# One 8 MB K load per head in place of two of 4 MB, with the second half copied aside

## The chip, the cores and the metric

The kernel runs on one core of one Trainium2 chip. The metric is the device time of one execution in microseconds; a kernel is timed in several rounds beside the kernel before on the same chip. Nothing here fell in a slow state, apart from one run of the kernel before (501.61 us, in the job of the last three edits to the changed kernel), which is left out of every ratio.

## The reference, cut to what matters

A decoder block for one token: a modulated layernorm, attention with 32 query heads over 4 cached KV heads and 32768 positions for 2 batches, an output projection, then an MLP. The caches are 8 pairs (batch, KV head) of an 8 MB K and an 8 MB V, 134 MB of the 178 MB that are read. "Head" below is such a pair; heads are counted from 0 to 7.

```python
q = (x @ wq).reshape(B, Sq, Hq, Dh).transpose(0, 2, 1, 3)      # B, Sq = 2, 1; Hq, Dh = 32, 128
k = jnp.repeat(k_cache, rep, axis=1)                           # k_cache: (2, 4, 32768, 128) bf16
scores = jnp.einsum('bhqd,bhkd->bhqk', q, k) * Dh ** (-0.5)
p = _softmax(scores, axis=-1)
o = jnp.einsum('bhqk,bhkd->bhqd', p, v)                        # v from v_cache, of k_cache's shape
return o.transpose(0, 2, 1, 3).reshape(B, Sq, Hq * Dh) @ wo
```

## The kernel before

SyncE issues all loads, in a fixed order, into an arena of 160 KB per partition. For a head there are two K slots of 32 KB and one V slot of 64 KB. A load waits until everything that read the slot has finished. Within a head, K is worked through in four chunks (cc) of eight groups (g8). A group is eight PE transposes of 128 x 128 into one of four PSUM buffers, an eviction to SBUF by VectorE or ScalarE, and eight small products with q, three groups later. The maximum of the scores, the exponential and the PV product follow when all four chunks are done. The kernel's own bookkeeping enters every read of a PSUM bank as a write, so two engines that read one bank take turns, in the order in which the program names them.

```python
EVAC_PATTERN = ("dve", "act", "dve", "act", "dve", "dve", "act", "dve")
def add_k(i, hf):
    add(("K", i, hf), [2, TPC * D], A_k_cache[i % 2, i // 2].rearrange(
        "(p h c t) d -> h p c (t d)", h=2, c=2, p=128)[hf], hf * 32 * KB, f"K{hf}")
def add_v(i):
    add(("V", i), [NCH, TPC * D], A_v_cache[...]..., 64 * KB, "V")
for i in range(NBG):
    add_k(i, 0)
    add_k(i, 1)
    add_v(i)
# ...
def tr(i, cc, g8):
    it = need("K", i, cc // 2)            # the half that holds this chunk
    kt = it.view[:, cc % 2, :]...
    for jj in range(8):
        pe(... e.transpose(psKT[kq][...], w[:, t, :], ident[:, :]), reads=[it.reg, "ident"], ...)
    # evict psKT to KT_sb[g8] on ScalarE or VectorE, by EVAC_PATTERN[g8]
def qk(i, cc, g8):
    # ... eight products into the bank psS[cc % 2]; after the last group of a chunk:
    act(... copy of the bank to S_sb ..., sem=f"sc{cc}")
    dve(... maximum of the bank to m1c ...)
```

Of the kernel before, what the change touches and what calls it, by code (L numbers as in the profile page):

```python
# [6 lines left out]
ALU = mybir.AluOpType  # L7
AX = mybir.AxisListType
BF16 = mybir.dt.bfloat16
FP32 = mybir.dt.float32  # L10

B, G, S, D = 2, 4, 32768, 128
HQ = 32
HPG = HQ // G
# [5 lines left out]
NBG = B * G  # L20
# [6 lines left out]
TPC = CH_ROWS // 128  # L27
NCH = S // CH_ROWS
# [3 lines left out]
PIPE = 3  # L32
NPKT = 4
RING = 160 * 1024
AHEAD = ("sc2", "sc3", "pk", "ac")
WMOD_ITEMS = ((0, 1), (1, 4), (4, 8))
W2_ITEMS = ((0, 8, 96), (8, 16, 112), (16, 24, 128), (24, 27, 144), (27, 28, 150))
EVAC_PATTERN = ("dve", "act", "dve", "act", "dve", "dve", "act", "dve")


class Tracker:
# [161 lines left out]
    def _loop(self, eng, E, body, bounds):  # L203
        pairs = [w[1:] for op in body for w in op[1]]
        often = [p for p in dict.fromkeys(pairs) if p != (1, 0) and pairs.count(p) > 1]
        with eng.Fori(*bounds) as it:
            val = {(1, 0): it}
            for step, off in often:
                val[step, off] = eng.snap(it * step + off)

            def wait(w):
                eng.wait_ge(self.sem[w[0]], val[w[1:]] if w[1:] in val else it * w[1] + w[2])

            for op in body:
                self._emit(eng, E, op, wait)
# [18 lines left out]
def bass_adaLN_cond__gqa_block_cached__mixer_channel_mlp__decode_kernel(  # L234
# [13 lines left out]
    out: bass.AP,  # L248
):
    T = Tracker(nc)  # L250
    T.step["pe"], T.step["dve"] = 72, 14

    def sb(name, shape, dtype=FP32):
        return nc.alloc_sbuf_tensor(name, list(shape), dtype)
# [1 line left out]
    ident = sb("ident", [128, 128], BF16)  # L256
# [14 lines left out]
    abase = nc.lookup_mloc(arena).addr  # L271
# [30 lines left out]
    m1c = sb("m1c", [128, HPG, NCH])  # L302
# [16 lines left out]
    psKT = [nc.alloc_psum_tensor(f"psKT{i}", [128, 1024], BF16) for i in range(NPKT)]  # L319
# [10 lines left out]
    stream = []  # L330
    by_key = {}
    views = {}
    KB = 1024

    def add(key, shape, src, off, slot=None):
        it = Item()
        it.key, it.n = key, len(stream)
        it.off, it.nbytes = off, int(np.prod(shape)) * 2
        assert off + it.nbytes <= RING
        it.reg = f"it{it.n}"  # L340
        it.sem = f"d_{slot or it.reg}"
        it.view = views.get(slot)
        if it.view is None:
            it.view = nc.alloc_sbuf_tensor_at(f"{key[0]}_{it.n}", [128] + list(shape), BF16, offset=abase + off)
            if slot:
                views[slot] = it.view
        it.src = src
        stream.append(it)
        by_key[key] = it

    def add_k(i, hf):
        add(("K", i, hf), [2, TPC * D], A_k_cache[i % 2, i // 2].rearrange("(p h c t) d -> h p c (t d)", h=2, c=2, p=128)[hf], hf * 32 * KB, f"K{hf}")

    def add_v(i):
        add(("V", i), [NCH, TPC * D], A_v_cache[i % 2, i // 2].rearrange("(p c t) d -> p c (t d)", c=NCH, p=128), 64 * KB, "V")
# [6 lines left out]
    for m in range(2):  # L362
        add(("wq", m), [4, HQ * D], wq_v[:, 4 * m:4 * m + 4, :], (96 + 32 * m) * KB)
    for i in range(NBG):
        add_k(i, 0)
        add_k(i, 1)
        add_v(i)
    for m, off in enumerate((128, 0)):
        add(("wo", m), [16, DM], A_wo[m * 2048:(m + 1) * 2048, :].rearrange("(p j) n -> p j n", j=16), off * KB)
    w1_v = B_w1.rearrange("(p k) n -> p k n", k=KT8)  # L370
    for m, off in enumerate((32, 64)):
        add(("w1", m), [4, F], w1_v[:, 4 * m:4 * m + 4, :], off * KB)
    w2_v = B_w2.rearrange("(p j) n -> p j n", j=FT)
    for m, (j0, j1, off) in enumerate(W2_ITEMS):
        add(("w2", m), [j1 - j0, DM], w2_v[:, j0:j1, :], off * KB)
    w2_of = {j: (m, j - j0) for m, (j0, j1, off) in enumerate(W2_ITEMS) for j in range(j0, j1)}

    pos = [0]

    def need(*key):  # L380
        it = by_key[key]
        while pos[0] <= it.n:
            cur = stream[pos[0]]
            old = [o.reg for o in stream[:cur.n] if o.off < cur.off + cur.nbytes and cur.off < o.off + o.nbytes]
            if len(cur.view.shape) == 3:
                dst = cur.view[:, :, :]
            else:
                dst = cur.view[:, :]
            T.dma("sp", lambda e, dst=dst, src=cur.src: e.dma_start(dst, src), key=cur.sem, writes=[cur.reg], frees=old)
            pos[0] += 1  # L390
        return it


    def dve(fn, reads=(), writes=(), sem=None):
        T.inst("dve", fn, reads=reads, writes=writes, sem=sem)

    def act(fn, reads=(), writes=(), sem=None):
        T.inst("act", fn, reads=reads, writes=writes, sem=sem)
# [16 lines left out]
    for k in range(KT8):  # L415
        pe(lambda e, k=k: e.matmul(psM[:, 2 * k:2 * k + 2], lhsT=c2[:, k::KT8], rhs=ident[0:2, 0:2], start=True, stop=True),
           reads=["KT_sb0", "ident"], writes=["psM"], mark=False)
# [46 lines left out]
    for k in range(KT8):  # L464
        k0, kk = wmod_of[k]
        it = need("wmod", k0)
        for ch in range(12):
            n, q = ch // 4, ch % 4
            pe(lambda e, w=it.view, k=k, kk=kk, ch=ch, n=n, q=q: e.matmul(bank[n][32 * q:32 * q + 32, :], lhsT=inT[:, k, :], rhs=w[:, kk, ch * 512:(ch + 1) * 512],  # L469
                                                                   start=(k == 0), stop=(k == KT8 - 1), skip_group_check=True),  # L470
               reads=[it.reg, "inT"], writes=[breg[n]], mark=(ch % 4 == 3))
# [6 lines left out]
    for n in range(3):  # L478
        for i in range(4):
            lo = 32 * n + 2 * i  # L480
            pe(lambda e, n=n, i=i, lo=lo: e.matmul(psM[:, lo:lo + 32].rearrange("p (q r) -> p q r", r=8)[:, :, 0:2],
                                                   lhsT=row[:, n * 512 + i * 128:n * 512 + (i + 1) * 128], rhs=idf, start=True, stop=True),
               reads=[f"mrow{n}", "identf"] + ROW, writes=["psM"], mark=(i == 3))
# [19 lines left out]
    for k in range(KT8):  # L503
        it = need("wq", k // 4)
        for ch in range(8):
            n, q = ch // 4, ch % 4
            pe(lambda e, w=it.view, k=k, ch=ch, n=n, q=q: e.matmul(bank[n][32 * q:32 * q + 32, :], lhsT=inT[:, k, :], rhs=w[:, k % 4, ch * 512:(ch + 1) * 512],
                                                                   start=(k == 0), stop=(k == KT8 - 1), skip_group_check=True),
               reads=[it.reg, "inT"], writes=[breg[n]], mark=(ch % 4 == 3))
    act(lambda e: e.activation(qrow[:, 0:512], bank[0][:, :], ACT.Copy), reads=[breg[0]], writes=["qrow0"] + EREG)  # L510
    dve(lambda e: e.tensor_copy(qrow[:, 512:1024], bank[1][:, :]), reads=[breg[1]], writes=["qrow1"] + EREG)
    for n in range(2):
        for i in range(4):
            pe(lambda e, n=n, i=i: e.matmul(psM[:, 0:64].rearrange("p (b h) -> p h b", b=2)[:, 16 * n + i:16 * n + 16:4, :],
                                            lhsT=qrow[:, n * 512 + i * 128:n * 512 + (i + 1) * 128], rhs=idr, start=True, stop=True),
               reads=[f"qrow{n}", "ident"] + EREG, writes=["psM"], mark=(i == 3))
    dve(lambda e: e.tensor_copy(qT[:, :, :], psM[:, 0:64].rearrange("p (b h) -> p b h", b=2)), reads=["psM"], writes=["qT"], sem="mo")

    for name in AHEAD:
        T.key(name, T.step.get(name, 1))  # L520
        T.raw("pe", lambda e, name=name: e.sem_inc(T.sem[name], T.step.get(name, 1)))
    T.wait("pe", reads=["ident", "identf", "onesf", "hmat"], writes=["psS0", "psS1", "psO", "psM"] + [f"psKT{q}" for q in range(NPKT)])

    pipe = []
# [3 lines left out]
        T.inst("pool", lambda e: e.tensor_copy(qcur[:, :], qT[:, b, g * HPG:(g + 1) * HPG]), reads=["qT"] + [f"atT{g}" for g in range(G // 2)], writes=["qcur"], sem="qc")  # L528

    def tr(i, cc, g8):  # L530
        it = need("K", i, cc // 2)
        kt = it.view[:, cc % 2, :].rearrange("p (t d) -> p t d", d=D)
        kq = g8 % NPKT
        for jj in range(8):
            t = g8 * 8 + jj
            pe(lambda e, kq=kq, jj=jj, w=kt, t=t: e.transpose(psKT[kq][:, jj * 128:(jj + 1) * 128], w[:, t, :], ident[:, :]),  # L536
               reads=[it.reg, "ident"], writes=[f"psKT{kq}"], mark=(jj == 7))
        src = psKT[kq][:, :].rearrange("p (a n) -> p a n", a=8)
        if EVAC_PATTERN[g8] == "act":
            act(lambda e, src=src: e.activation(KT_sb[g8][:, :, :], src, ACT.Copy), reads=[f"psKT{kq}"], writes=[f"KT_sb{g8}"], sem=f"ev{cc}_{g8}")  # L540
        else:
            dve(lambda e, src=src: e.tensor_copy(KT_sb[g8][:, :, :], src), reads=[f"psKT{kq}"], writes=[f"KT_sb{g8}"], sem=f"ev{cc}_{g8}")  # L542

    def qk(i, cc, g8):
        ps, preg = psS[cc % 2], f"psS{cc % 2}"
        for jj in range(8):
            t = g8 * 8 + jj
            pe(lambda e, t=t, jj=jj: e.matmul(ps[:, t * HPG:(t + 1) * HPG], lhsT=KT_sb[g8][:, jj, :], rhs=qcur[:, :], start=True, stop=True),  # L548
               reads=[f"KT_sb{g8}", "qcur"], writes=[preg], mark=(jj == 7))
        if g8 == TPC // 8 - 1:  # L550
            Sc = S_sb[:, :, cc * TPC:(cc + 1) * TPC]
            act(lambda e: e.activation(Sc, ps.rearrange("p (t h) -> p h t", h=HPG), ACT.Copy), reads=[preg], writes=[f"S_sb_{cc}"], sem=f"sc{cc}")  # L552
            dve(lambda e: e.tensor_reduce(m1c[:, :, cc], ps.rearrange("p (t h) -> p h t", h=HPG), AX.X, ALU.max), reads=[preg], writes=[f"m1c{cc}"])  # L553

    def softmax_1():
        dve(lambda e: e.tensor_reduce(m1[:, :], m1c[:, :, :], AX.X, ALU.max), reads=[f"m1c{cc}" for cc in range(NCH)], writes=["m1"], sem="m1")  # L556
# [62 lines left out]
    for i in range(NBG):  # L619
        T.segments = rounds[i + 1] = {E: [] for E in T.LOOPED}  # L620

        for cc in range(NCH):
            for g8 in range(TPC // 8):
                tr(i, cc, g8)
                pipe.append((i, cc, g8))
                if (cc, g8) == (0, 0):
                    next_q(i)
                if len(pipe) > PIPE:
                    qk(*pipe.pop(0))
        while pipe:  # L630
            qk(*pipe.pop(0))
        softmax_1()
        softmax_2()
        softmax_3()
        for cc in range(NCH):
            exp(cc)
        for cc in range(NCH):
            part_sum(cc)
            pv(i, cc)
        row_sums()  # L640
        extract()
        extract_2(i)
        T.segments = None
# [6 lines left out]
    for m in range(2):  # L650
        it = need("wo", m)
        for j in range(16):
            for hf in range(2):
# [3 lines left out]
                   reads=[it.reg, f"atT{m}"], writes=["psS0"], mark=(j == 15 and hf == 1))  # L657
# [27 lines left out]
    for q in range(4):  # L685
        for n in range(2):
# [3 lines left out]
               reads=["b1m", "ident"], writes=[zreg[n]], mark=False)  # L690
    for k in range(KT8):
        it = need("w1", k // 4)
        for n in range(2):
            for q in range(4):
                lo = 896 * q + 448 * n
                pe(lambda e, w=it.view, k=k, n=n, q=q, lo=lo: e.matmul(zbank[n][32 * q:32 * q + 32, 0:448], lhsT=inT[:, k, :], rhs=w[:, k % 4, lo:lo + 448],
                                                                       start=False, stop=(k == KT8 - 1), skip_group_check=True),
                   reads=[it.reg, "inT"], writes=[zreg[n]], mark=(q == 3))
        if k == 1:
            pe(lambda e: e.matmul(psM[:, 44:52], lhsT=b2m[:, :], rhs=ident[0:KT8, 0:KT8], start=True, stop=True),  # L700
               reads=["b2m0", "b2m1", "b2m3", "b2m7", "ident"], writes=["psM"])
# [3 lines left out]
        reads=["psS1", "psO"], writes=["zrow"] + ROW)  # L705
# [3 lines left out]
        reads=["z2", "zrow"] + ROW, writes=["z2"])  # L709
# [5 lines left out]
    for g in range(16):  # L715
        m, j = w2_of[g]
        it = need("w2", m)
        for hf in range(2):
            t = 2 * (g % 2) + hf
# [5 lines left out]
    for g in range(16, FT):  # L725
        m, j = w2_of[g]
# [46 lines left out]
```

## Time and profile before

| what | value |
|---|---|
| median time | 420.12 us (420.05 to 420.14, 3 runs) |
| span of the profiled run | 418.7 us |
| busy: PE, VectorE, ScalarE | 70%, 50%, 36% |
| loads | 178.28 MB, the queue busy 98.8% |
| V landing to the next V landing | 38.7 us |

The main lines stand in the prediction. Four more are needed later. The first two are groups of instructions, with count, busy time and mean duration in ns, then idle time before them; the other two, from the view of waits, give who waited for whom, for how long in total, how often, and the longest wait.

```profile
L540 ACT ACTIVATE KT_sb<-psKT 128x1024 bf16<-128x1024 bf16 x96 | 98.2, 1025 | 124.4 <-PE psKT L536 124.4
L542 DVE COPY KT_sb<-psKT 128x1024 bf16<-128x1024 bf16 x160 | 106.7, 688 | 61.6 <-PE psKT L536 61.2
...
PE psZ L584 <- DMA V<-in_A_v_cache_dram: 20.0, 6, 4.5
...
ACT S_sb L552 <- PE psZ L548: 7.5, 9, 1.4
```

Both evicting engines idle for PE and PE waits for V: compute has room. ScalarE's copy of a score bank (L552) hardly waits.

### The profile page before, as it was taken

How to read it: one execution, taken by the hardware profiler on the slowest of the kernel's cores; microseconds unless marked ns; L12 is line 12 of the kernel's file. 1: busy time of each engine (PE TensorE's matmuls, PEld its weight loads, DVE VectorE, ACT ScalarE, POOL GpSimd, SP SyncE). 2: the span in 40 equal slices, each digit the busy share in tenths (PEclk: the TensorE clock that was granted, in tenths of full speed). 3: DMA queues.
4: the chain of work that ended last, by engine and by line, in shares of the span. 5: the costliest groups of instructions: out<-in, count | busy, mean ns of one | idle time of the engine just before them, and what ended most of it. 6: DMA issues, size and time to landing. Idle time of an engine off the chain costs nothing.

```text
span 418.7 us, 11609 instructions
## 1 busy us (share of the span) xinstructions
PE 291.0 (70%) x5183; PEld 231.3 (55%) x5183; DVE 209.6 (50%) x423; ACT 149.4 (36%) x179; POOL 6.8 (2%) x29
## 2 busy tenths in 40 slices
PE   1407449766996895699369957976995699564536
PEld 1104219762993794299149926962894399221214
DVE  1201105546677676467726664766477567620411
ACT  2000015533565364256405632643365166400100
POOL 3000000000000000000000000000000000000000
PEclk9999557986896997799589958986697889576585
DMA  9989999999999999999999999999999999899995
GB/s 373 450 380 449 448 404 493 398 406 446 441 432 429 423 451 429 419 454 457 391 435 476 407 416 448 438 438 426 438 438 426 416 460 457 377 448 428 424 427 249
DMA packets 5581, 178.42 MB, mean 426 GB/s; under 512 B 698, under 2 KB 706, under 8 KB 964
## 3 DMA queue, kind: packets, MB, share of 16 engines
q1 hardware_dynamic: 5572, 178.28, 98.8%
q8 instruction: 8, 0.13, 0.1%
q14 instruction: 1, 0.01, 0.0%
HBM read 178.28 MB, written 0.00 MB: 426 GB/s over the span
## 4 chain that ended last, share of the span: by engine, by line
DMA 71%; PE 24%; DVE 2%; issue 1%; ACT 1%; SPq 1%
DMA V<-in_A_v_cache_dram 39%; DMA wo<-in_A_wo_dram 10%; DMA K<-in_A_k_cache_dram 10%; PE psZ L584 10%; DMA w<-in_B_w_dram 9%; PE psKT L536 8%; DMA wmod<-in_w_mod_dram 4%; PE psS L548 1%; PE psZ L548 1%; PE psS L655 1%; PE psZ L729 1%; PE psZ L469 1%; ACT KT_sb L540 0%; PE psS L469 0%; DVE m1c L553 0%
## 5 line engine op out<-in xcount | busy, mean ns | idle before, releaser
L536 PE MATMUL psKT<-ident,K 128*128 128x128 bf16 x2048 | 163.1, 229 | 11.5 <-DMA K<-in_A_k_cache_dram 11.5
L540 ACT ACTIVATE KT_sb<-psKT 128x1024 bf16<-128x1024 bf16 x96 | 98.2, 1025 | 124.4 <-PE psKT L536 124.4
L542 DVE COPY KT_sb<-psKT 128x1024 bf16<-128x1024 bf16 x160 | 106.7, 688 | 61.6 <-PE psKT L536 61.2
L536 PEld LDWEIGHTS psKT<-ident,K 128*128 128x128 bf16 x2048 | 126.7, 102 | 13.0 <-DMA K<-in_A_k_cache_dram 12.7
L584 PE MATMUL psZ<-V,E_sb 128*32 128x512 bf16 x512 | 46.4, 541 | 23.2 <-DMA V<-in_A_v_cache_dram 20.0
L548 PE MATMUL psS<-qcur,KT_sb 128*128 128x8 bf16 x1024 | 44.7, 167 | 2.2 <-issue 2.2
L584 PEld LDWEIGHTS psZ<-V,E_sb 128*32 128x32 bf16 x512 | 18.7, 130 | 47.7 <-issue 38.8
L548 PE MATMUL psZ<-qcur,KT_sb 128*128 128x8 bf16 x1024 | 43.0, 167 | 2.2 <-issue 1.5
L548 PEld LDWEIGHTS psS<-qcur,KT_sb 128*128 128x128 bf16 x1024 | 40.0, 97 | 2.3 <-issue 2.3
L548 PEld LDWEIGHTS psZ<-qcur,KT_sb 128*128 128x128 bf16 x1024 | 37.9, 96 | 3.4 <-issue 1.6
L572 ACT ACTIVATE E_sb<-S_sb 128x512 bf16<-128x512 f32 x32 | 19.5, 630 | 29.6 <-DVE S_sb L570 29.6
L570 DVE TENSOR_TENSOR S_sb<-S_sb,gmb 128x512 f32<-128x512 f32 x32 | 20.0, 685 | 0.3
L576 DVE TENSOR_REDUCE rs<-E_sb 128x8 f32<-128x512 bf16 x32 | 19.7, 675 | 0.0
L469 PE MATMUL psS<-wmod,inT 128*32 128x512 bf16 x32 | 5.1, 624 | 16.2 <-DMA wmod<-in_w_mod_dram 16.2
L553 DVE TENSOR_REDUCE m1c<-psZ 128x8 f32<-128x512 f32 x16 | 11.1, 693 | 10.2 <-ACT S_sb L552 10.1
L595 DVE RECIPROCAL rinv<-psM 128x1 f32<-128x1 f32 x8 | 1.3, 168 | 27.7 <-PE psM L593 27.7
L605 PE MATMUL psM<-msum,hmat 128*128 128x128 f32 x16 | 4.2, 347 | 13.3 <-DVE msum L600 13.3
L559 PE MATMUL psM<-identf,m 128*8 128x128 f32 x16 | 4.3, 369 | 13.1 <-DVE m L556 13.1
L553 DVE TENSOR_REDUCE m1c<-psS 128x8 f32<-128x512 f32 x16 | 11.1, 693 | 3.2 <-ACT S_sb L552 3.1
L552 ACT ACTIVATE S_sb<-psZ 128x512 f32<-128x512 f32 x16 | 9.5, 595 | 7.5 <-PE psZ L548 7.5
L477 DVE COPY S_sb<-psS 128x512 f32<-128x512 f32 x1 | 0.7, 690 | 22.9 <-PE psS L469 22.9
L469 PEld LDWEIGHTS psS<-wmod,inT 128*32 128x32 bf16 x32 | 1.1, 132 | 19.3 <-DMA wmod<-in_w_mod_dram 18.0
(123 smaller groups left out, 167.5 us busy)
## 6 DMA issues: line engine op xcount, KB each, us to landing
K<-in_A_k_cache_dram SPq DMA_DIRECT2D x16, 4096.0 KB, 27.1
wq<-in_A_wq_dram SPq DMA_DIRECT2D x2, 4096.0 KB, 44.8
wo<-in_A_wo_dram SPq DMA_DIRECT2D x2, 4096.0 KB, 39.0
w<-in_B_w_dram SPq DMA_DIRECT2D x2, 3584.0 KB, 32.5
wmod<-in_w_mod_dram SPq DMA_DIRECT2D x1, 6144.0 KB, 29.8
w<-in_B_w_dram SPq DMA_DIRECT2D x3, 2048.0 KB, 37.8
wmod<-in_w_mod_dram SPq DMA_DIRECT2D x1, 4608.0 KB, 15.8
wmod<-in_w_mod_dram SPq DMA_DIRECT2D x1, 1536.0 KB, 6.0
```

Of the source, the lines that this page charges most:

```text
L469: pe(lambda e, w=it.view, k=k, kk=kk, ch=ch, n=n, q=q: e.matmul(bank[n][32 * q:32 * q + 32, :], lhsT=inT[:, k, :], rhs=w[:, kk, ch * 512:( ...
L536: pe(lambda e, kq=kq, jj=jj, w=kt, t=t: e.transpose(psKT[kq][:, jj * 128:(jj + 1) * 128], w[:, t, :], ident[:, :]), reads=[it.reg, "ident" ...
L540: act(lambda e, src=src: e.activation(KT_sb[g8][:, :, :], src, ACT.Copy), reads=[f"psKT{kq}"], writes=[f"KT_sb{g8}"], sem=f"ev{cc}_{g8}")
L542: dve(lambda e, src=src: e.tensor_copy(KT_sb[g8][:, :, :], src), reads=[f"psKT{kq}"], writes=[f"KT_sb{g8}"], sem=f"ev{cc}_{g8}")
L548: pe(lambda e, t=t, jj=jj: e.matmul(ps[:, t * HPG:(t + 1) * HPG], lhsT=KT_sb[g8][:, jj, :], rhs=qcur[:, :], start=True, stop=True), reads= ...
L552: act(lambda e: e.activation(Sc, ps.rearrange("p (t h) -> p h t", h=HPG), ACT.Copy), reads=[preg], writes=[f"S_sb_{cc}"], sem=f"sc{cc}")
L553: dve(lambda e: e.tensor_reduce(m1c[:, :, cc], ps.rearrange("p (t h) -> p h t", h=HPG), AX.X, ALU.max), reads=[preg], writes=[f"m1c{cc}"])
L559: pe(lambda e: e.matmul(psM[0:HPG, 0:128], lhsT=m1[:, :], rhs=identf[:, :], start=True, stop=True), reads=["m1", "identf"], writes=["psM"])
L570: dve(lambda e: e.tensor_tensor(Sc, Sc, gmb[:, :].unsqueeze(2).to_broadcast([128, HPG, TPC]), ALU.subtract), reads=[f"S_sb_{cc}", "gmb"], ...
L572: act(lambda e: e.activation(Ec, Sc.rearrange("p h (u t) -> p u h t", t=4), ACT.Exp, scale=SCALE), reads=[f"S_sb_{cc}"], writes=[f"E_sb_{c ...
L576: dve(lambda e: e.tensor_reduce(rs4[:, :, cc], Ec.rearrange("p u h t -> p h u t"), AX.XY, ALU.add), reads=[f"E_sb_{cc}"], writes=[f"rs4_{c ...
L584: pe(lambda e, t4=t4, tg=tg, q=q: e.matmul(psO[32 * q:32 * q + 32, :], lhsT=E_sb[:, tg // 4, :, :].rearrange("p h t -> p (h t)"), rhs=vt[: ...
```

## The change

K of a head becomes one 8 MB load into one 64 KB slot. So that the slot comes free when only half of K has been transposed, VectorE copies the second half into a 32 KB area of its own (kc) while PE works on the first half. Chunks 2 and 3 are transposed from that area. Only head 0 keeps two loads, so that PE can begin it early. In the first half of a head one eviction per chunk moves from VectorE to ScalarE; the maximum of a bank now comes before ScalarE's copy of it. Weights of the tail change their places in the arena.

```diff
-EVAC_PATTERN = ("dve", "act", "dve", "act", "dve", "dve", "act", "dve")
+EVAC_PATTERN = (("dve", "act") * 4, ("dve", "act", "dve", "act", "dve", "dve", "act", "dve"))
+    def add_k(i):
+        rows = A_k_cache[i % 2, i // 2].rearrange("(p c t) d -> p c (t d)", c=NCH, p=128)
+        if i:
+            add(("K", i), [NCH, TPC * D], rows, 0, "K", view=kv)
+            by_key["K2", i] = by_key["K", i]
+        else:
+            add(("K", i), [2, TPC * D], rows[:, 0:2, :], 0, sem="K", view=kv[:, 0:2, :])
+            add(("K2", i), [2, TPC * D], rows[:, 2:4, :], 32 * KB, sem="K2", view=kv[:, 2:4, :])
 ...
     def tr(i, cc, g8):
-        it = need("K", i, cc // 2)
-        kt = it.view[:, cc % 2, :].rearrange("p (t d) -> p t d", d=D)
+        it = need("K", i)
+        kt = (kv[:, cc, :] if cc < 2 else kc[:, cc - 2, :]).rearrange("p (t d) -> p t d", d=D)
+        k_reg = it.reg if cc < 2 else f"kc{2 * (cc - 2) + g8 // 4}"
 ...
+    def keep(i, n):
+        it = need("K2", i)
+        lo = n % 2 * 32 * D
+        dve(lambda e: e.tensor_copy(kc[:, n // 2, lo:lo + 32 * D], kv[:, 2 + n // 2, lo:lo + 32 * D]), reads=[it.reg], writes=[f"kc{n}"], sem=f"kc{n}")
 ...
+            dve(lambda e: e.tensor_reduce(m1c[:, :, cc], ...), reads=[preg], writes=[f"m1c{cc}"], sem=f"mc{cc}")
             act(lambda e: e.activation(Sc, ...), reads=[preg], writes=[f"S_sb_{cc}"], sem=f"sc{cc}")
-            dve(lambda e: e.tensor_reduce(m1c[:, :, cc], ...), reads=[preg], writes=[f"m1c{cc}"])
 ...
                 tr(i, cc, g8)
+                if cc < 2 and g8 % 4 == 1:
+                    keep(i, 2 * cc + g8 // 4)
```

More of the change, by code (lines that the diff above doesn't have):

```diff
@@ L34 @@
 RING = 160 * 1024
+KC_AT = 128 * 1024
 AHEAD = ("sc2", "sc3", "pk", "ac")
 WMOD_ITEMS = ((0, 1), (1, 4), (4, 8))
-W2_ITEMS = ((0, 8, 96), (8, 16, 112), (16, 24, 128), (24, 27, 144), (27, 28, 150))
-EVAC_PATTERN = ("dve", "act", "dve", "act", "dve", "dve", "act", "dve")
+W2_ITEMS = ((0, 8, 96), (8, 16, 112), (16, 24, 0), (24, 27, 16), (27, 28, 22))
+EVAC_PATTERN = (("dve", "act") * 4, ("dve", "act", "dve", "act", "dve", "dve", "act", "dve"))
 class Tracker:
@@ L211, in wait @@
             def wait(w):
+                if w[1] == 0:
+                    return eng.wait_ge(self.sem[w[0]], w[2])
                 eng.wait_ge(self.sem[w[0]], val[w[1:]] if w[1:] in val else it * w[1] + w[2])
@@ L250, in bass_adaLN_cond__gqa_block_cached__mixer_channel_mlp__decode_kernel @@
     T = Tracker(nc)
-    T.step["pe"], T.step["dve"] = 72, 14
+    T.step["pe"], T.step["dve"] = 72, 10
     def sb(name, shape, dtype=FP32):
@@ L333, in bass_adaLN_cond__gqa_block_cached__mixer_channel_mlp__decode_kernel, with add @@
     KB = 1024
-    def add(key, shape, src, off, slot=None):
+    def add(key, shape, src, off, slot=None, sem=None, view=None):
         it = Item()
@@ L340, in add @@
         it.reg = f"it{it.n}"
-        it.sem = f"d_{slot or it.reg}"
-        it.view = views.get(slot)
+        it.sem = f"d_{sem or slot or it.reg}"
+        it.view = views.get(slot) if view is None else view
         if it.view is None:
@@ L349, in add @@
         by_key[key] = it
-    def add_k(i, hf):
-        add(("K", i, hf), [2, TPC * D], A_k_cache[i % 2, i // 2].rearrange("(p h c t) d -> h p c (t d)", h=2, c=2, p=128)[hf], hf * 32 * KB, f"K{hf}")
+    kv = nc.alloc_sbuf_tensor_at("kv", [128, NCH, TPC * D], BF16, offset=abase)
+    def add_k(i):
[6 more added lines that the diff above has]
+            add(("K2", i), [2, TPC * D], rows[:, 2:4, :], 32 * KB, sem="K2", view=kv[:, 2:4, :])
+            T.key("d_K2")
+            T.step["d_K2"] = 0
     def add_v(i):
@@ L364, in bass_adaLN_cond__gqa_block_cached__mixer_channel_mlp__decode_kernel @@
     for i in range(NBG):
-        add_k(i, 0)
-        add_k(i, 1)
+        add_k(i)
         add_v(i)
-    for m, off in enumerate((128, 0)):
+    for m, off in enumerate((0, 32)):
         add(("wo", m), [16, DM], A_wo[m * 2048:(m + 1) * 2048, :].rearrange("(p j) n -> p j n", j=16), off * KB)
     w1_v = B_w1.rearrange("(p k) n -> p k n", k=KT8)
-    for m, off in enumerate((32, 64)):
+    for m, off in enumerate((128, 64)):
         add(("w1", m), [4, F], w1_v[:, 4 * m:4 * m + 4, :], off * KB)
@@ L376, in bass_adaLN_cond__gqa_block_cached__mixer_channel_mlp__decode_kernel @@
     w2_of = {j: (m, j - j0) for m, (j0, j1, off) in enumerate(W2_ITEMS) for j in range(j0, j1)}
+    kc = nc.alloc_sbuf_tensor_at("kc", [128, 2, TPC * D], BF16, offset=abase + KC_AT)
     pos = [0]
@@ L384, in need @@
             old = [o.reg for o in stream[:cur.n] if o.off < cur.off + cur.nbytes and cur.off < o.off + o.nbytes]
+            if cur.n > by_key["V", NBG - 1].n and cur.off < KC_AT + 32 * KB and KC_AT < cur.off + cur.nbytes:
+                old += [f"kc{n}" for n in range(4)]
             if len(cur.view.shape) == 3:
@@ L521, in bass_adaLN_cond__gqa_block_cached__mixer_channel_mlp__decode_kernel @@
         T.raw("pe", lambda e, name=name: e.sem_inc(T.sem[name], T.step.get(name, 1)))
+    T.wait("dve", writes=[it.reg for it in stream if it.key[0] in ("wmod", "wq")])
     T.wait("pe", reads=["ident", "identf", "onesf", "hmat"], writes=["psS0", "psS1", "psO", "psM"] + [f"psKT{q}" for q in range(NPKT)])
@@ L536, in tr @@
             pe(lambda e, kq=kq, jj=jj, w=kt, t=t: e.transpose(psKT[kq][:, jj * 128:(jj + 1) * 128], w[:, t, :], ident[:, :]),
-               reads=[it.reg, "ident"], writes=[f"psKT{kq}"], mark=(jj == 7))
+               reads=[k_reg, "ident"], writes=[f"psKT{kq}"], mark=(jj == 7))
         src = psKT[kq][:, :].rearrange("p (a n) -> p a n", a=8)
-        if EVAC_PATTERN[g8] == "act":
+        if EVAC_PATTERN[cc // 2][g8] == "act":
             act(lambda e, src=src: e.activation(KT_sb[g8][:, :, :], src, ACT.Copy), reads=[f"psKT{kq}"], writes=[f"KT_sb{g8}"], sem=f"ev{cc}_{g8}")
@@ L551, in qk @@
             Sc = S_sb[:, :, cc * TPC:(cc + 1) * TPC]
+            dve(lambda e: e.tensor_reduce(m1c[:, :, cc], ps.rearrange("p (t h) -> p h t", h=HPG), AX.X, ALU.max), reads=[preg], writes=[f"m1c{cc}"], sem=f"mc{cc}")
             act(lambda e: e.activation(Sc, ps.rearrange("p (t h) -> p h t", h=HPG), ACT.Copy), reads=[preg], writes=[f"S_sb_{cc}"], sem=f"sc{cc}")
-            dve(lambda e: e.tensor_reduce(m1c[:, :, cc], ps.rearrange("p (t h) -> p h t", h=HPG), AX.X, ALU.max), reads=[preg], writes=[f"m1c{cc}"])
     def softmax_1():
```

## The prediction

> **What bounds the kernel now.** I first read the page's slices and queues, to see whether any engine or the DMA is full all the time. The row of digits is the busy share of each fortieth of the span.
>
> ```profile
> DMA  9989999999999999999999999999999999899995
> q1 hardware_dynamic: 5572, 178.28, 98.8%
> HBM read 178.28 MB, written 0.00 MB: 426 GB/s over the span
> ```
>
> Every slice of the DMA row but the last is 8 or 9, while PE is busy 70% and VectorE 50% of the span. 178.28 MB in one queue at 98.8% is a kernel bound by its loads. Next the chain that ended last, in order of time, from head 1 to head 3:
>
> ```profile
> 116.98 0.47 PE psKT L536 x8
> ...
> 132.72 5.19 PE psZ L584 x62
> 137.91 0.05 PE psM L593
> 137.97 31.01 DMA V<-in_A_v_cache_dram
> 168.97 0.14 issue
> 169.11 5.76 PE psZ L584 x62
> 174.92 32.74 DMA V<-in_A_v_cache_dram
> 207.66 0.14 issue
> 207.79 5.20 PE psZ L584 x49
> 213.04 33.25 DMA V<-in_A_v_cache_dram
> 246.29 0.14 issue
> ```
>
> From head 2 on nothing but V transfers and the PV product between them is on the path; the period is 207.66 - 168.97 = 38.69 us and 246.29 - 207.66 = 38.63 us for 16.78 MB, or 434 GB/s. The 31 to 33 us of a V load are mostly standing in line. The DMA issues in order of time, with each issue's time to landing, show the line (the second K half was issued at 198.7):
>
> ```profile
> 174.92 0.33 SPq L389 DMA_DIRECT2D V<-in_A_v_cache_dram  x1
> 188.40 10.68 SPq L389 DMA_DIRECT2D K<-in_A_k_cache_dram  x2
> 213.04 0.33 SPq L389 DMA_DIRECT2D V<-in_A_v_cache_dram  x1
> ...
> DMA to landing us min/median/max: 28.2/28.2/28.2
> ```
>
> The second K half of head 4 lands at 198.7 + 28.2 = 226.9, 19.2 us after V of head 3; V of head 4 lands 19.4 us later, at 246.3. So two 4 MB loads with 32 KB per partition move as fast as one 8 MB load with 64 KB. Averaged over heads 2 to 7 I get 19.3 us for each kind. The reader should see that there is no gap between landings, and no rate to win from a larger load.
>
> **What the skill says.** "DMA: Bandwidth & Descriptors", Specifications, gives a fabric ceiling of 435 GB/s; the 434 GB/s of the loop agrees, so the loads already run at it. The same page, Latency and other measured facts, puts first byte of a load from SyncE at about 0.6 us; the trace has no direct figure, but the 4 KB output takes 1.4 us from issue to landing. I use 1 to 2 us as the dead time if the queue ever runs dry. "VectorE: DVE Perf Modes", the perf-mode tier table, has a bf16 copy inside SBUF at 4 elements a cycle (693 ns for 2048, about 150 cycles of it fixed), and at most 2 with PSUM as source. The trace agrees with the second: 1024 elements from PSUM take 688 ns, and (512 + 150) / 0.96 is 690. No SBUF copy of this kind is in the trace, so the new copy is an estimate from that page: 4096 / 4 = 1024 cycles, plus 150, over 0.96 = 1.22 us. "SBUF — State Buffer", SBUF: two separate sides, says that compute and DMA use separate ports, so I take no slowdown of the loads from the copies; no run here shows it yet.
>
> **The change part by part.**
> (1) Loads. Seven heads' K goes from two 4 MB loads to one of 8 MB. Same bytes, same addresses, same rate: 0 us, and seven DMA issues fewer, which were never waited for.
> (2) When K can be used. Before, PE began a head when the first half landed; now it begins when all 8 MB have, one half (19.3 / 2 = 9.65 us) later. This is no time by itself, since the path is the queue, but it uses up the slack that kept the queue full.
> (3) Copies. Four of 1.22 us a head are 4.9 us more of VectorE; in the first half of a head two evictions of 688 ns move to ScalarE (1025 ns each there). VectorE in that half: 8 x 0.69 + 4.9 + one maximum 0.69 = 11.1 us, where before it had 6.6 us in the 9.75 us of a half (178.65 to 188.40, with PE at full clock). Three other halves with PE cold took 11.0 to 12.0 us. So VectorE now sets the pace of the first half: about 12.5 to 13 us in place of a mean of 11. +1.7 us a head on the compute chain, -0.6 us because the score maximum no longer waits for ScalarE's copy of the same bank (L552, 0.60 us on the chain before L553).
> (4) Is the queue still full? First half 12.7, second half 10.3 (188.40 to 198.70, unchanged), then until the end of PV without a wait for V, from head 1: 137.97 - 126.5 = 11.5; the PV product varied from 5.2 to 6.4, so 11.9 on average. Sum 12.7 + 10.3 + 11.9 - 0.6 = 34.3 us from K landing to the issue of the next V. The queue holds work until the next K has landed, 38.7 us after this one: 4.4 us of slack, some 2.5 us after dead time. The next K is issued 12.7 us after landing, when V of the head (19.3 us) is still moving: 6.6 us of slack. Before the slack was 14 us for V (33.3 - 19.3) and 19 us for K. Thin, but positive: 0 us in steady state, perhaps 0.5 for a head that comes late.
> (5) The first head. VectorE's order is eviction, copy, eviction, and the first copy waits for the second half of K, which lands at 37.4 + 34.9 = 72.3 us; the head began at 62.45. VectorE stands still until then, so PE gets through six groups and stops. After 72.3: four copies 4.9, seven evictions 4.8, a maximum 0.7, small gaps 0.4 = 10.8 us, so the first half ends at 83.1 and not at 74.49 (the next K's issue). The rest took 102.47 - 74.49 = 28.0 us and should again, less 0.6: V of head 1 is issued at 83.1 + 28.0 - 0.6 = 110.5. K of head 1 lands at 111.0 (90.1 + 20.9). With the dead time, the queue is empty for about 1.2 us, once; everything after moves by that much.
> (6) The tail. The output projection and MLP weights now take slots of K, of the copy and of V. K's slot is free at 343 + 13 = 356, V of head 7 moves until 362; wo is read by 386 at the latest, and the last w2 pieces in its place are due in the queue after 400. The final weights still land last: 0 us.
> Sum: 420.1 + 1.2 (first head) + 0.5 (a late head) = 421.8 us.
>
> **Rivals.**
> A, larger loads move faster. For it speaks only the intent. Against it, the landings above: equal, at the ceiling. All the ideal could give is 178.28 MB at 435 GB/s, 409.8 us, plus start and tail; of that the K loads of seven heads are a third. I give it next to nothing; at the most 418.
> B, the compute chain becomes the bound. If the copy ran at 2 elements a cycle (estimate (2048 + 150) / 0.96 = 2.3 us), VectorE gets 4.3 us more in each first half, the chain is 38.6 us, and with dead time each of seven heads is 2 to 3 us late: 437 to 441 us. Against it: source and target lie in SBUF, are bf16 and run without stride. A milder form, a chain of 36 to 37 us from a cold PE and waits for the four PSUM buffers, gives 0.5 to 1 us a head: 424 to 428.
> C, the first head costs more than (5). The trace has two stalls of PE there (1.49 and 2.24 us, labelled issue). If they grow, or the start of VectorE after 72.3 is slower, V is issued 2 to 4 us late: 423 to 426. If they shrink, the cost is nil and the time stays at 420.
>
> **Range and chances.** The middle is (1) to (6) with the first head's small hole, 421.8. The low end 419.6 is no hole at all and a slightly better tail; the high end 427 is rival C with some of the milder B. Faster by over 2% needs under 411.7 us, which the ceiling forbids in practice: 0.01. Slower by over 2% needs over 428.5, so B in some form: 0.08. Within 2%: 0.91.
>
> **What would show it.** Right: DMA row still 8 and 9, apart from a dip between 100 and 120 us; V landings 38.7 us apart; PE waits for K for about 4 us at each head and hardly for V; the copy's mean near 1.2 us; K loads landing in 19.3 us after V. Wrong: V or K issued after the previous load has landed in heads 2 to 7 (B), a copy of over 2 us (B), first V over 3 us after 111 us (C), or a K load that takes clearly less than 19.3 us of the queue (A).

## The result, and the profile after

The changed kernel takes 424.56 us (422.55 to 426.45, 4 runs); before, in the same rounds, 420.13 us. The ratio is 1.0105, with a 95% interval of 1.0057 to 1.0153. A ratio is the mean time of one kernel's fast runs over that of the other's of the same rounds, so it is not quite the ratio of the medians. It is within 2%, but slower by 4.4 us where 1.7 was forecast. New, too, is the spread: 3.9 us between runs, where the kernel before has 0.2.

The page of the kernel after shows almost nothing of it: the slices look full, and the queue's share fell by 0.6 points.

```profile
DMA  9999999999999999999999999999999999999994
...
q1 hardware_dynamic: 4564, 178.28, 98.2%
```

The DMA issues of heads 3 and 4 after the change, in order of time (start, duration), and the time to landing of the last two of them (each from the view of the loaded tensor):

```profile
184.87 0.33 SPq L404 DMA_DIRECT2D V<-in_A_v_cache_dram  x1
200.77 0.33 SPq L404 DMA_DIRECT2D kv<-in_A_k_cache_dram  x1
224.28 0.33 SPq L404 DMA_DIRECT2D V<-in_A_v_cache_dram  x1
239.45 0.33 SPq L404 DMA_DIRECT2D kv<-in_A_k_cache_dram  x1
...
DMA to landing us min/median/max: 23.9/23.9/23.9
...
DMA to landing us min/median/max: 28.1/28.1/28.1
```

K of head 4 was issued at 200.77, and the chain below has it 26.43 us long, so it landed at 227.20. V of head 4 was issued at 224.28, 2.9 us earlier, and landed at 248.2. That is 21.0 us after K, where every V load of the loop before took 19.3 to 19.4. The next K, issued in good time, landed 19.4 us later. V of head 6 lost 2.0 us in the same way (21.3 us), V of head 2 lost 0.3. K of head 7 lands at 346.8 and not at 343.0: nearly all of this profiled run's 4.1 us (422.8 - 418.7) is there, before the tail.

The chain that ended last, in head 4 after the change:

```profile
200.77 26.43 DMA kv<-in_A_k_cache_dram
...
227.25 3.45 PE psKT L553 x32
...
234.58 0.74 DVE kc L564
...
235.71 0.68 DVE KT_sb L559
236.39 0.61 DVE m1c L574
...
237.52 1.03 ACT KT_sb L557
...
238.59 0.35 PE psZ L570 x8
238.95 0.47 PE psKT L553 x8
...
239.45 28.07 DMA kv<-in_A_k_cache_dram
```

Before, the path in the loop was V, PV, V. Now a head is: K lands, PE transposes it, a copy, an eviction, a maximum and another eviction follow one another on VectorE and ScalarE, and only then is the next K issued. 28 us of the load are still mostly standing in line, so the chain alone does not say which link costs time. Two more lines after the change, a group and a wait:

```profile
L564 DVE COPY kc<-kv 128x4096 bf16<-128x4096 bf16 x32 | 39.0, 1217 | 7.9 <-DMA kv<-in_A_k_cache_dram 7.9
...
ACT S_sb L575 <- DVE m1c L574: 42.9, 32, 2.4
```

A copy takes 1217 ns, as estimated. ScalarE now waits 42.9 us in all for VectorE's maximum, at each of the 32 banks.

**The 16 engines.** A load is split over 16 DMA engines; the trace records 16 times at which one of them has finished its part, but not which one. From that record I took, for V of heads 1 to 7, how long before the first and the last engine finished the load in front V was issued, and how long after that V landed, from first to first and from last to last. The first of one load need not be the first of the next. A selection, sorted by the first column, in us:

| kernel, head | issue before first engine done | before last | V on first engine | V on last engine |
|---|---|---|---|---|
| copies twice, 2 | -1.26 | 1.19 | 22.48 | 20.81 |
| copies twice, 4 | -0.95 | 0.43 | 22.39 | 21.26 |
| copies twice, 3 | 0.48 | 1.27 | 20.58 | 20.99 |
| after, 6 | 0.91 | 3.17 | 20.78 | 21.32 |
| after, 1 | 0.91 | 2.68 | 20.38 | 19.39 |
| after, 4 | 2.02 | 2.92 | 19.59 | 20.95 |
| after, 3 | 2.69 | 3.69 | 19.43 | 19.32 |
| after, 7 | 3.09 | 5.90 | 19.34 | 19.38 |
| before, 1 | 6.74 | 8.54 | 19.34 | 19.30 |
| before, 4 | 12.25 | 13.92 | 19.31 | 19.33 |

19.3 us is the load itself. On the first engine the excess is near 2 us less the lead: 1.1 to 1.5 at 0.91 of lead, 0.3 at 2.02, 0.1 at 2.69, nothing above 3, and 3.2 at -1.26. (In the experiments below single V loads still lost 0.5 us at 2.8 and 0.25 us at 3.9.) So time is lost unless the next load is issued some 2 to 3 us before the first engine runs out. Over all K and V loads issued after 80 us in the 13 traces, the last landing goes the same way: the median loss is 1.4 us with under 1 us of such lead (12 loads), 1.0 with 1 to 2 us (9) and 0.05 with 2 to 3 us (18, of which one lost 1.6).

The first engine runs out 0.8 to 2.8 us before the last one after the change (1.7 to 1.8 in the loop before). This spread lasts: an engine that has lost time keeps its own queue of later loads and stays behind (K of head 5 shows the 2.3 us that V of head 4 opened). A load counts as landed when the last engine has it, so losing engines cost little while they are the early ones (head 1 after the change), and cost all when they are the late ones. Which engine loses, this lead does not tell. The packets of V of head 4, put into 16 chains by their times, show that 14 engines lost at most 0.5 us, and that two which ran out among the last, 2.5 us after the issue, lost 1.0 and 1.7 us. These two made the landing late; why these two is open.

### The profile page after: what moved, and what is told of

It is laid out like the page before. It is cut to its first block, busy times and chain, and to the rows that moved or that the text cites. A ratio compares the mean times of both kernels' runs of the same rounds, so it can differ in the third digit from the quotient of the medians.

```text
span 422.8 us, 11626 instructions
## 1 busy us (share of the span) xinstructions
PE 298.8 (71%) x5183; PEld 233.4 (55%) x5183; DVE 233.9 (55%) x439; ACT 165.7 (39%) x195; POOL 6.8 (2%) x29
## 4 chain that ended last, share of the span: by engine, by line
DMA 67%; PE 20%; DVE 5%; issue 3%; ACT 3%; SPq 0%; ACTq 0%; DVEq 0%
DMA kv<-in_A_k_cache_dram 53%; PE psKT L553 13%; DMA wmod<-in_w_mod_dram 7%; DMA w<-in_B_w_dram 7%; ACT KT_sb L557 2%; PE psS L570 2%; DVE m1c L574 2%; DVE KT_sb L559 2%; PE psZ L606 1%; DVE kc L564 1%; PE psZ L570 1%; PE psS L679 1%; PE psZ L484 1%; PE psZ L753 1%; PE psS L484 0%
## 5 line engine op out<-in xcount | busy, mean ns | idle before, releaser
L557 ACT ACTIVATE KT_sb<-psKT 128x1024 bf16<-128x1024 bf16 x112 | 111.9, 1024 | 102.1 <-PE psKT L553 102.1
L559 DVE COPY KT_sb<-psKT 128x1024 bf16<-128x1024 bf16 x144 | 98.1, 690 | 61.5 <-PE psKT L553 61.4
L553 PE MATMUL psKT<-ident,kv 128*128 128x128 bf16 x1024 | 89.3, 246 | 15.1 <-DMA kv<-in_A_k_cache_dram 15.1
L553 PEld LDWEIGHTS psKT<-ident,kv 128*128 128x128 bf16 x1024 | 72.2, 112 | 16.6 <-DMA kv<-in_A_k_cache_dram 16.6
L553 PE MATMUL psKT<-ident,kc 128*128 128x128 bf16 x1024 | 77.7, 218 | 0.0
L553 PEld LDWEIGHTS psKT<-ident,kc 128*128 128x128 bf16 x1024 | 58.2, 97 | 0.0
L606 PE MATMUL psZ<-V,E_sb 128*32 128x512 bf16 x512 | 48.8, 565 | 13.2 <-ACT E_sb L594 13.2
L570 PEld LDWEIGHTS psS<-qcur,KT_sb 128*128 128x128 bf16 x1024 | 40.2, 98 | 12.2 <-DVE KT_sb L559 6.7
L570 PEld LDWEIGHTS psZ<-qcur,KT_sb 128*128 128x128 bf16 x1024 | 36.5, 96 | 13.6 <-ACT KT_sb L557 11.1
L564 DVE COPY kc<-kv 128x4096 bf16<-128x4096 bf16 x32 | 39.0, 1217 | 7.9 <-DMA kv<-in_A_k_cache_dram 7.9
L575 ACT ACTIVATE S_sb<-psS 128x512 f32<-128x512 f32 x16 | 9.6, 597 | 20.2 <-DVE m1c L574 20.2
## 6 DMA issues: line engine op xcount, KB each, us to landing
wo<-in_A_wo_dram SPq DMA_DIRECT2D x2, 4096.0 KB, 21.5
```

The costliest lines, as they stand in the source:

```text
L553: pe(lambda e, kq=kq, jj=jj, w=kt, t=t: e.transpose(psKT[kq][:, jj * 128:(jj + 1) * 128], w[:, t, :], ident[:, :]), reads=[k_reg, "ident"] ...
L557: act(lambda e, src=src: e.activation(KT_sb[g8][:, :, :], src, ACT.Copy), reads=[f"psKT{kq}"], writes=[f"KT_sb{g8}"], sem=f"ev{cc}_{g8}")
L559: dve(lambda e, src=src: e.tensor_copy(KT_sb[g8][:, :, :], src), reads=[f"psKT{kq}"], writes=[f"KT_sb{g8}"], sem=f"ev{cc}_{g8}")
L564: dve(lambda e: e.tensor_copy(kc[:, n // 2, lo:lo + 32 * D], kv[:, 2 + n // 2, lo:lo + 32 * D]), reads=[it.reg], writes=[f"kc{n}"], sem=f" ...
L570: pe(lambda e, t=t, jj=jj: e.matmul(ps[:, t * HPG:(t + 1) * HPG], lhsT=KT_sb[g8][:, jj, :], rhs=qcur[:, :], start=True, stop=True), reads= ...
L575: act(lambda e: e.activation(Sc, ps.rearrange("p (t h) -> p h t", h=HPG), ACT.Copy), reads=[preg], writes=[f"S_sb_{cc}"], sem=f"sc{cc}")
```

## The experiments

Theory 1: V is issued too late, when PE must wait for all of K and works longer on it; the queue runs thin. Theory 2: the copies in SBUF slow the loads. Theory 3: an 8 MB K load is itself worse. All runs passed the check of the result, even one whose result is wrong on purpose, which is told.

**V in two loads.** The changed kernel; V of a head as two loads of 4 MB, so that its first half is issued when half of the PV product is done.

```diff
-        add(("V", i), [NCH, TPC * D], A_v_cache[...], 64 * KB, "V")
+        for h in range(2):
+            add(("V", i, h), [2, TPC * D], rows[:, 2 * h:2 * h + 2, :], (64 + 32 * h) * KB, f"V{h}")
 ...
-        it = need("V", i)
+        it = need("V", i, cc // 2)
```

> The changed kernel, with V of each head as two loads of 4 MB, each into half of V's slot; the first is issued when half of the PV product is done, about 2.9 us earlier than the whole load (half of 5.8 us). Theory 1 (V is issued with only 3 us of loads left in the queue, and the 16 DMA engines do not run out together): slack grows from 3.5 to 6.4 us, so 420.1 to 421.0 us and a spread of the runs under 0.5 us. Theory 2 (the copies in SBUF slow the loads) and theory 3 (an 8 MB K load is itself worse than two of 4 MB): unchanged, 423 to 426 us.

Measured: 420.21 us (420.18 to 420.36, 5 runs), ratio 1.0002 [0.9989, 1.0015]. Both the loss and the spread are gone, with the 8 MB K loads and the copies in place. The issues of heads 4 and 5 in this run:

```profile
220.64 2.80 SPq L406 DMA_DIRECT2D V<-in_A_v_cache_dram  x2
240.01 0.33 SPq L406 DMA_DIRECT2D kv<-in_A_k_cache_dram  x1
260.61 3.29 SPq L406 DMA_DIRECT2D V<-in_A_v_cache_dram  x2
```

The first V half of head 4 leaves at 220.64; K of that head landed at 227.0, 6.4 us later. Over heads 2 to 7 it leaves 32.9 us after the K before has landed, where the changed kernel needs 35.2. Theories 2 and 3 fall here.

**K in two loads, PE waits for both.**

```diff
-        if i: add(("K", i), [NCH, ...], rows, 0, "K", view=kv) ... else: two loads
+        add(("K", i), [2, TPC * D], rows[:, 0:2, :], 0, sem="K", view=kv[:, 0:2, :])
+        add(("K2", i), [2, TPC * D], rows[:, 2:4, :], 32 * KB, sem="K2", view=kv[:, 2:4, :])
 ...
+        both = [need("K2", i).reg] if cc == 0 else []      # read by the transposes of chunk 0
```

> The changed kernel, but K of every head comes as two loads of 4 MB as before, and PE waits for both before it begins a head; copies as they are. Theory 1: the slack of V stays at about 3.5 us, so 423 to 426 us with the spread of the changed kernel. Theory 2: the same 423 to 426. Theory 3: back to 420.1 to 420.8.

Measured: 424.27 us (422.91 to 426.15, 6 runs), ratio 1.0109 [1.0087, 1.0130]: as the changed kernel. The size of the load is no part of the cost.

**Copies that nobody reads.** K in two loads, transposes from K's slot as before, the four copies made in the second half of each head and left unread; the two patterns of evictions are swapped with them.

```diff
-        kt = (kv[:, cc, :] if cc < 2 else kc[:, cc - 2, :])...
+        kt = kv[:, cc, :]...                                # it = need("K" if cc < 2 else "K2", i)
-                if cc < 2 and g8 % 4 == 1: keep(i, 2 * cc + g8 // 4)
+                if cc > 1 and g8 % 4 == 1: keep(i, 2 * (cc - 2) + g8 // 4)
```

> K of every head as two loads, PE begins at the first and reads both halves from K's slot as before; the four copies a head are still made, from the second half, but nobody reads them. Theory 1: PE begins a half earlier, slack of V about 13 us, so 420.1 to 421.0 in spite of the copies. Theory 2: the copies still slow the loads, 423 to 425. Theory 3: 420.1 to 421.

Measured: 420.08 us (420.01 to 420.21, 5 runs), ratio 0.9999 [0.9986, 1.0012]. The copies did run:

```profile
L560 DVE COPY kc<-kv 128x4096 bf16<-128x4096 bf16 x32 | 38.9, 1216 | 0.0
```

32 copies of 1.2 us in SBUF, beside a queue at its ceiling, cost the loads nothing. The separate ports that the prediction quotes now have a number beside them.

**Copies twice.** The slope: each copy is made two times.

```diff
+        for _ in range(2):
             dve(lambda e: e.tensor_copy(kc[...], kv[...]), ...)
```

> The changed kernel with each copy made twice: 4.9 us more of VectorE in the first half of each head. Theory 1: from K's landing to the next V's issue 35.2 becomes 40.1 us, more than the 38.7 us that the queue holds; with about 1 us of dead time every head takes 41 to 41.5 us, seven heads late by 2.4 to 2.8 us: 437 to 441 us. Theory 2: twice the cost of one set of copies, 428 to 429. Theory 3: 424 if the queue still hides it.

Measured: 435.77 us (433.67 to 436.33, 4 runs), ratio 1.0364. Not 428, which theory 2 gave; 1.2 us short of theory 1's range. From K's landing to V's issue it takes 40.0 us (forecast 40.1). K lands 40.8 us apart on average (151.6 for head 2 to 355.4 for head 7, over 5), where 41 to 41.5 was forecast. That the early engines go on and so hide a part of the dead time is likely, and not shown.

**No copies.** One 8 MB load, all transposes from K's slot.

```diff
-        kt = (kv[:, cc, :] if cc < 2 else kc[:, cc - 2, :])...
+        kt = kv[:, cc, :]...
-                if cc < 2 and g8 % 4 == 1: keep(i, 2 * cc + g8 // 4)
```

> The changed kernel without the copies: all transposes read K's slot, which is then free for the next K only after the last of them, about 21.5 us after K's landing, where V of the head keeps the queue busy for 19.3 us. Theory 1 in its general form (each load has to be issued about 3 us before the one in front ends): K is issued about 2 us after V's end, 3 to 3.5 us lost a head, 441 to 446 us. Theory 2 (the copies are the cost): 420.1 to 421.

Measured: 468.97 us (468.47 to 471.54, 5 runs), ratio 1.1167. The direction is that of theory 1, the size twice the forecast. Page, DMA issues and time to landing of the K issued at 182.77:

```profile
DMA  9999999989929994998699669968994999599995
...
182.77 0.33 SPq L402 DMA_DIRECT2D kv<-in_A_k_cache_dram  x1
...
DMA to landing us min/median/max: 21.9/21.9/21.9
```

Here the holes are in plain sight: one before K of each of heads 2 to 7, and one of 4.9 us before the weights of the output projection (V of head 7 landed at 405.2, their load left at 410.1), which the forecast had not counted. K of head 2 landed at 159.4, V at 178.7, and the next K was issued at 182.8: 4.1 us of empty queue, because 23.4 us of work were needed where I had put 21.5. Then an 8 MB load into an empty queue needs 21.9 us in place of 19.3: 2.6 us of dead time, where I had put 1 to 1.5. Both terms were too small. Without the copies the one-slot scheme costs 49 us.

**The kernel before, PE waits for both K halves.**

```diff
+        both = [need("K", i, 1).reg] if cc == 0 else []     # read by the transposes of chunk 0
```

> The kernel before with one wait more: PE begins a head only when both halves of K have landed. No copies, two loads of 4 MB. From landing to the next V's issue about 33 us, slack 5.7 us. Theory 1: hidden, 420.1 to 421. If waiting for the whole of K costs by itself, whatever the slack: 423 to 426.

Measured: 423.07 us (422.96 to 425.65, 5 runs), ratio 1.0080 [1.0066, 1.0094]. The forecast of theory 1 missed by 2 us, and the trace says where. In head 0 this kernel cannot even begin until 72.2 us, so the second K half of head 1 is issued at 98.5; the first engine finished the half in front at 99.4, and the second half lands at 113.4 in place of 111.0. V of head 1, issued 0.2 us before the first engine ran out, adds 1.3 us. In heads 2 to 7 no V loses over 0.3 us; they are issued 4.3 to 6.7 us before K has landed. So theory 1 stands, but I had forgotten head 0. The profiled run is the longest of the five (span 424.4; its state is fast), so the split of the typical 3 us is only indicated.

**Half of each copy** (the result is wrong on purpose: the other half of the area keeps old data, which the check of the result did not notice).

```diff
-kc[:, n // 2, lo:lo + 32 * D], kv[:, 2 + n // 2, lo:lo + 32 * D]
+kc[:, n // 2, lo:lo + 16 * D], kv[:, 2 + n // 2, lo:lo + 16 * D]
```

> The changed kernel, each copy cut to half of its columns (the result is wrong on purpose: the other half of the copy keeps old data). Theory 1 as the runs so far sharpen it (V must be issued some 2 us before the first of the 16 engines has finished K, and that engine is 1 to 3 us ahead of the last): VectorE has about 2.1 us less in the first half of a head, PE cold needs 11 us there anyway, so V is issued 1.2 to 1.5 us earlier: 420.2 to 421.8 us. If the lateness came from elsewhere (the single wait for all of K): 423 to 426 as the changed kernel.

Measured: 422.75 us (421.25 to 424.38, 6 runs), ratio 1.0070 [1.0049, 1.0092]: better (clear of the changed kernel's interval in the second job below, not of the wide one in its first), but outside of the 420.2 to 421.8 forecast. From K's landing to V's issue it is 34.8 us, only 0.4 less, and the first half takes 12.2 us where it took 12.4. So VectorE's load is not what sets the pace of the first half.

**Evictions as before.**

```diff
-EVAC_PATTERN = (("dve", "act") * 4, ("dve", "act", "dve", "act", "dve", "dve", "act", "dve"))
+EVAC_PATTERN = (("dve", "act", "dve", "act", "dve", "dve", "act", "dve"),) * 2
```

> The changed kernel, with the eviction pattern of the first half of a head as before (5 of 8 on VectorE, not 4): one part of the change undone. Theory 1: VectorE, which sets the pace there, gets two evictions, 1.4 us, more a head; V is issued about 1.2 us later, with about 1 us before the first engine runs out: 1 to 1.3 us more lost at each of seven heads, 428 to 432 us. If VectorE does not set the pace: 423 to 426.

Measured: 425.69 us (424.42 to 426.75, 5 runs), ratio 1.0124 [1.0106, 1.0141]. Expected 428 to 432: a miss for the same reason. 1.4 us more of VectorE a head make the chain 0.4 us longer (35.6); in time the run cannot be told from the changed kernel, whose interval overlaps.

**The maximum after ScalarE's copy.**

```diff
-            dve(... maximum of the bank ...)
             act(... copy of the bank ...)
+            dve(... maximum of the bank ...)
```

> The changed kernel, with the score maximum of each bank again after ScalarE's copy of it, as before: another part undone. Theory 1: 0.6 us later a head on the chain from K to V's issue, seven times some 0.3 to 0.6 us: 425.5 to 428.5 us. If that order is off the path: 423 to 426.

Measured: 422.98 us (421.01 to 425.44, 6 runs), ratio 1.0072 [1.0047, 1.0098]. I expected it to be slower; it is faster. The chain from K's landing to V's issue falls from 35.2 to 33.8 us. The wait of ScalarE shows why:

```profile
ACT S_sb L574 <- PE psZ L570: 6.1, 8, 0.8
```

The 42.9 us of waiting for the maximum are gone; VectorE now waits 11.7 us for ScalarE's copies instead. Each engine's stream is in order, and the kernel lets one reader at a time into a bank: with the maximum first, ScalarE stands before its copy until VectorE has come through its own copies and evictions, and the eviction behind it, for which PE waits, stands too.

**The changed kernel again, and both repairs together.** The last edit is the one of V's halves plus the one above.

> The changed kernel as it is, again, beside the next one on the same chip: 424.3 us, runs between 422 and 427. From K's landing to the next V's issue 35.2 us on average in the trace.

> V as two loads (which brought 420.2 alone) and the maximum again after ScalarE's copy (which in the last trace made the chain from K to V's issue 33.8 us in place of 35.2). Theory 1: no load is late, 420.0 to 420.4 us, spread under 0.4 us: as the kernel before and not faster, because the loads already run at the ceiling. If the order of the maximum had a worth beyond lateness: under 419.8.

Measured in one job: the changed kernel 425.03 us (422.93 to 425.77, 6 runs), ratio 1.0122 [1.0109, 1.0136], which does not overlap the ratio with the maximum moved back; its chain was again 35.2 us. Both repairs together 420.00 us (419.90 to 420.13, 5 runs), ratio 1.0000 [0.9986, 1.0014]. No late load, no gain: the version that loses nothing is as fast as the kernel before and not faster. None of the kernels beats it.

The runs beside one another. The middle column is from the profiled run of each: K's landing in heads 1 to 6 to the issue of V (the first half of V, where it has two) of the next head, mean. The two columns go together at the ends; between 33.8 and 35.2 their order is not strict.

| kernel | K landed to next V issued, us | median, us |
|---|---|---|
| V in two loads | 32.9 | 420.21 |
| maximum after the copy | 33.8 | 422.98 |
| before, PE waits for both | 33.8 | 423.07 |
| half of each copy | 34.8 | 422.75 |
| K in two loads, PE waits | 34.9 | 424.27 |
| changed kernel (two jobs) | 35.2 | 424.56, 425.03 |
| evictions as before | 35.6 | 425.69 |
| copies twice | 40.0 | 435.77 |

## Why the prediction was right or wrong

The time fell into the range, and the verdict of no gain at the ceiling held; the middle was 2.8 us too low. That the range held is in part luck: its high end was set by a dear first head (rival C) with some of the milder B, and the first head cost nothing. The loss came from the loop, to which the middle gave 0.5 us.

1. *Loads move at the same rate (part 1, rival A).* Right. K lands 19.3 to 19.4 us after V as one load or two, and the edit with two K loads took the changed kernel's time.
2. *PE begins a half later, which costs slack and no time by itself (part 2).* Right. Two V loads gave back a lead of 2.3 us, and with it all of the time.
3. *+1.7 us for the first half, -0.6 us for the order of the maximum (part 3).* The copy was right (1217 ns for 1.22 us), and so was the size of the first half: 12.4 us on average for 12.5 to 13 (11.5 in the kernel before with the added wait). Its reason, that VectorE sets the pace, was not: half the copies shorten it by 0.2 us. Made twice, they do set it (16.9 us). The -0.6 had the wrong sign. I counted one dependency of L553 that vanished, and not the one that appeared for ScalarE; going back to the old order is worth 1.4 us a head on the chain.
4. *34.3 us, so 4.4 us of slack, 2.5 after dead time, "0 us in steady state, perhaps 0.5" (part 4).* This is the step that failed. The chain is 35.2 us and the slack 3.5. The dead time is 2 to 2.6 us and not 1 to 2. And it has to be kept before the first of 16 engines runs out, not before the load has landed; that engine is 0.8 to 2.8 us ahead. Slack and need are then equal within a microsecond. The 0.5 us measured 3.7 in the profiled run (346.75 - 343.02). Which heads lose is decided by fractions of a microsecond. One source is the PV product, which took 5.0 us in head 2 at a granted clock of 0.72 and 6.5 in head 3, just before the late V of head 4, at 0.55. The first 32 transposes are none here: in head 3 they were the quickest, 2.9 us where heads 1, 2 and 5 took 3.6. What makes the spread between runs was not tested.
5. *The first head, 1.2 us (part 5).* The first half ended at 83.4 us (forecast 83.1). But V of head 1 was issued at 108.3, not 110.5: the two stalls of PE had shrunk from 3.7 us to one of 1.3. The last engine lost nothing there: 0 us in place of 1.2.
6. *The tail costs nothing (part 6).* Right: 53.7 us from V of head 7 to the last weights, 53.4 before.

Of the rivals, the milder form of B comes nearest: its 424 to 428 us held, and the loss is 0.6 us a head on average. But it named a chain of 36 to 37 us, and at 35.2 us the loss came from a need for slack that it did not name; in the profiled run nearly all of it fell on heads 4 and 6.

## What to carry to other kernels

In a kernel that is bound by its loads, a change that moves no bytes is judged by the lead of each load: issue time against the moment when the first DMA engine has finished the load in front, and not by the queue's share of busy time, which hardly moved here. Here about 5 us of lead before landing were enough (2 to 3 for the issue, the rest for the spread of the engines): with 5 us or more, no K or V load of the 13 traces lost over 0.4 us. If a slot comes free too late, split its load so that the first half can leave early. Where two engines read one bank in turn, ask which of them has work queued behind that others wait for, and let that one go first.

## What the Trainium skill lacked or had wrong

- "DMA: Bandwidth & Descriptors", Anatomy of one DMA: it gives a fixed cost of some 2 us per DMA, mostly completion, for DMAs that GpSimd issues (here SyncE does), and does not say when loads in front hide it. Here next to nothing was lost with over 3 us of lead before the first engine ran out (0.05 us in the median of 21 loads with 3 to 4 us). With less, the first landing loses about the missing part (1.1 to 1.5 us at 0.9 us of lead), and into an empty queue an 8 MB load takes 21.9 us for 19.3.
- The same page says that the engines of one DMA finish independently, but not how far apart or for how long: 1.7 us in the kernel before, all but unchanged over 300 us, and up to 3.0 us in the kernel after, where a spread once opened stayed (2.3 us in V of head 4 and still in K of head 5).
- The same page, Bandwidth, says that for transfers from HBM the HBM side, about 358 GB/s, binds. Its own note there limits this: about 358 is what each core gets when both cores of a pair stream. Read alone, the sentence misleads: in this kernel, which runs on one core, the loop reads HBM at 434 GB/s, by the page's own figure the fabric ceiling.
- No page that I read says which of two readers of one PSUM bank should go first where they take turns: 42.9 us of waiting in ScalarE and 1.4 us a head on the chain came from letting VectorE go first.
